# Turning B and C of the later pairs on TensorE instead of by DMA, in a fused state-space scan and bilinear feed-forward kernel

## The chip, the cores and the metric

One core of a Trainium2 chip. The metric is the device time of one execution in microseconds; the kernel before has a median of 124.77 us over three runs. An engine's work is named as the profile names it: PE is TensorE, DVE is VectorE, ACT is ScalarE, POOL is GpSimd, SP is SyncE.

## What is computed

Four batches of eight heads, 768 tokens each; x has 32 channels a head, B and C have 16 states. Blocked over tokens, the reference is

```python
cum = np.cumsum(log(a))                      # within a block of tokens
M   = (C_blk @ B_blk.T) * causal * exp(cum_i - cum_j)
y   = M @ x_blk + (C_blk @ state) * exp(cum_i)
state = exp(cum_last) * state + (B_blk * exp(cum_last - cum_j)).T @ x_blk
# heads side by side: 256 columns a token, 3072 tokens
out = ((y @ w_a) * (y @ w_b)) @ w_out        # 256 -> 1536 -> 256
```

## The kernel before

**Blocks and pairs.** A block is 128 tokens of all four batches; there are six (0 to 5). A pair is two of the four batches in one block, so pairs 0 to 11, two for each block; `P0 = 4` is the first pair of block 2 and `P2 = 8` the first of block 4. The decays are turned into factors for B and C (`fB`, `fC`, from TensorE's `factors_mm`, L254; for pairs from P2 on `fBl`, `fCl`, from VectorE's `late_factors`, L277), so that scores are plain products of scaled B (`bm`) and scaled C (`cm`). G, the decay over a block's border, comes from one matmul (L815).

**Rows.** Below P2 a partition holds two neighbouring tokens of one batch (`i r` in the code): B and C load in pieces of 128 bytes, x in 256. From P2 on a partition holds one token of both batches: pieces of 64 and 128 bytes, twice as many, loaded by one DMA for both batches (L163), not one for each (L154).

**A pair's way.** POOL scales B and C (`scale_bc`, L304 and L312). For the scores B and C must be turned, states to partitions, with odd and even heads of B in separate copies. Pairs 0 to 3 are turned by TensorE (`transposes`, four 128x128 transposes into PSUM, L334); ScalarE copies B twice, once for each head parity (`bt`, L345), VectorE copies C (`ct`, L346). Pairs 4 to 11 are turned by DMA (`turn`): POOL lays B's two parities and C out in a tile `planes` (L304, two copies at L322) and SP issues one transposing DMA from it (L356). Then come the scores (`scores`, L388, from P2 on L373), the causal mask (`mask`: three products on VectorE, one by ScalarE's copy `tmp` and POOL), the products with x and the part from the state, the sums for the next state (DS), and the copy to the feed-forward's input.

**Feed-forward.** Blocks 0 and 1 go pair by pair (`unit`: two k's of 128 hidden columns, four matmuls for `aps`, four for `bps`; ScalarE copies aps to `asb`, VectorE multiplies into `hk`; `out_half`: twelve matmuls and a copy `osb`). From block 2 on both pairs of a block go together: `group` does the state part (L523), products (L448 or L433) and DS (L475 or L462) of two pairs, ScalarE copies the result to `XB` (L553); `bunit` is one k with 512 columns (two matmuls each for aps and bps), `bout` one of four output halves (L709).

**What sets the order.** Everything is recorded in one hand-written order (`manual_schedule`); each engine takes its instructions in that order. PSUM has four banks for SC (scores, products, DS) and four that aps, bps, ops and the like share; a string `BANKS` gives, digit by digit, which of the four each new tile gets, so a tile waits until the copy of the tile before it in that bank is done. Input tiles have three buffers each (`inp`), output tiles ten. Loads stand on POOL's queue (weights with a cast, early pairs) and SP's (the rest); stores on SP. Stores of blocks 0 and 1 are collected in `stores` and issued at once in block 3. The order around the later blocks is

```python
masked(7, (0, 1, 2), *bu(2, 5, 6, 7, 8, 9, 10, 11))
group(3)
bout(2, 0)
bout(2, 1)
stage(8, True, (6, 7))        # scores(8), masks
...
masked(8, (2,), *bu(3, 0, 1, 2, 3, 4, 5))
for blk in range(4, NBLK):    # scores, bout(blk-2, 2), units 6 to 9, group(blk), bout(blk-2, 3), units 10, 11
```

Of the kernel before, what the change touches and what calls it, by code (L numbers as in the profile page):

```python
# [22 lines left out]
    "032130132013201320120310231023120132031203120132013201320310213021320310231023120130231023"  # L23
    "1021320312031203123021302130213021302130213021031203120312031203120312031203120312031"
# [4 lines left out]
def kernel(  # L29
# [28 lines left out]
    P2 = 8  # L58
# [4 lines left out]
    p32 = np.zeros((BH, 128 + nb * NG), np.float32)  # L63
    p32[:, 0:128] = (bh[:, None] % H) == (j[None, :] // N)
# [9 lines left out]
    c32 = const.tile([BH, p32.shape[1]], f32, name="c32")  # L74
# [5 lines left out]
    selb = c32[:, 128 : 128 + nb * NG]  # L80
# [8 lines left out]
    Wb = [big.tile([128, 2, KC], f16, name=f"Wb{t}") for t in range(2)]  # L89
# [7 lines left out]
    planes = [big.tile([128, 6, H * N], f16, name=f"planes{t}") for t in range(2)]  # L97
    causal_q = big.tile([128, Q], f16, name="causal_q")
    causal_r = big.tile([128, 2, Q], f16, name="causal_r")
# [5 lines left out]
    NL = NBLK - P2 // NBP  # L105
# [5 lines left out]
    hsx = big.tile([BH, nb, NG], f32, name="hsx")  # L111
    G = big.tile([128, nb, NG], f32, name="G")

    inp = ctx.enter_context(tc.tile_pool(name="inp", bufs=3))
# [31 lines left out]
    def load1(eng, p, which, bt, i0=0, n=64):  # L146
        blk, bp = divmod(p, NBP)
        if p >= P2:
            return eng.dma_start(
                by_token(pair_in[p][which])[:, bt],  # L150
                (B, C, x)[which][2 * bp + bt, :, blk * Q : (blk + 1) * Q, :].rearrange("h q n -> q h n"),
            )
        src = (B, C, x)[which][2 * bp + bt, :, blk * Q + 2 * i0 : blk * Q + 2 * i0 + 2 * n, :]
        return eng.dma_start(  # L154
            pair_in[p][which][64 * bt + i0 : 64 * bt + i0 + n].rearrange("i h r n -> i h (r n)"),
            src.rearrange("h (i r) n -> i h (r n)", r=2),
        )

    def load2(eng, p, which):
        if p < P2:  # L160
# [7 lines left out]
    def load_w(half):  # L168
        c = slice(half * KC, (half + 1) * KC)
        return [  # L170
            nc.gpsimd.dma_start(W[half], src.rearrange("(f p) e -> p f e", p=128)[:, :, c])
            for W, src in ((Wa, moe_w_a), (Wb, moe_w_b))
        ]
# [22 lines left out]
    nc.vector.memset(zero, 0.0)  # L196
    nc.gpsimd.memset(sel, 1.0)
# [22 lines left out]
    load_w(0)  # L220
# [48 lines left out]
    def late_rows(eng):  # L269
        k0 = P2 // NBP  # L270
# [14 lines left out]

    def scale_x(p, eng):
# [3 lines left out]
        if eng is nc.scalar:  # L290
# [4 lines left out]
    def scale_bc(p, which, eng, factor=None):  # L295
        blk, bp = divmod(p, NBP)
        name, f = (("bm", fB), ("cm", fC))[which]
        if p >= P2:
            f = (fBl, fCl)[which][:, blk - P2 // NBP].rearrange("p (b t h) -> p b t h", b=NBP, t=2)[:, bp]
        else:  # L300
            f = f[:, blk, :, bp]
        raw = by_token(pair_in[p][which]) if p >= P2 else pair_in[p][which].rearrange("p h r n -> p r h n")
        if p >= P0 and which:
            eng.tensor_tensor(  # L304
                out=planes[p % 2][:, 4:6].rearrange("p t (h n) -> p t h n", n=N),
                in0=raw,
                in1=f.unsqueeze(3).broadcast_to((128, 2, H, N)),
                op=ALU.mult,
            )
            return  # L310
# [8 lines left out]
        if p >= P0:  # L319
            dst = planes[p % 2][:, 0:4].rearrange("p (t e) (m f n) -> p t e m f n", e=2, f=2, n=N)  # L320
            for e in range(2):
                eng.tensor_copy(dst[:, :, e, :, e], m_.rearrange("p t (m f) n -> p t m f n", f=2)[:, :, :, e])  # L322

    def transposes(p, ps=None, between=None, apart=False):
        s = st[p]
        if ps is None:
            ps = [SC[0], SC[1]] if apart else None
            on_dve = apart
        else:
            on_dve = True  # L330
        TB, TC = (TT[:, 0:256], TT[:, 256:512]) if ps is None else [t_.bitcast(f16)[:, 0:256] for t_ in ps]
# [11 lines left out]
        for e in range(2):  # L343
            o_ = BT[:, e].rearrange("p r t i -> p (r t i)")
            b_.append(nc.scalar.activation(out=o_, in_=TB, func=AF.Copy, scale=par[:, e : e + 1]))  # L345
        c_ = (nc.vector.tensor_copy if on_dve else nc.scalar.copy)(  # L346
# [7 lines left out]
    def turn(p):  # L354
        T_ = mid.tile([128, 6, 128], f16, name="turned", tag="turned")
        nc.sync.dma_start(T_, planes[p % 2].rearrange("p a c -> p (a c)"), transpose=True)  # L356
        if p >= P2:
            st[p]["BT"] = T_[:, 0:4].rearrange("p (t e) k -> p e t k", e=2)
            st[p]["CT"] = T_[:, 4:6]
        else:  # L360
            st[p]["BT"] = T_[:, 0:4].rearrange("p (r e) (t i) -> p e r t i", e=2, t=2)
            st[p]["CT"] = T_[:, 4:6].rearrange("p r (t i) -> p t r i", t=2)

    def shaped(t_, p):
        return t_.rearrange("p (r i) -> p r i", r=2) if P0 <= p < P2 else t_

    def scores(p):
        BT, CT = st[p]["BT"], st[p]["CT"]
        st[p]["T1"] = mid.tile([128, H, 2, Q], f16, name="t1", tag="t1")
        for e, bt, m in itertools.product(range(2), range(2), range(4)) if p >= P2 else ():  # L370
# [11 lines left out]
        for e in range(2) if p < P2 else ():  # L382
            for r in range(2):
                for m in range(4):
                    for bt in range(2):
# [3 lines left out]
                            shaped(SC[m][64 * bt : 64 * bt + 64, c0 : c0 + Q], p),  # L389
# [8 lines left out]
    def product(p, m):  # L398

        if p >= P2:  # L400
# [8 lines left out]
            (causal_r if p >= P0 else causal).rearrange("p r q -> p (r q)").unsqueeze(1).broadcast_to((128, 2, 2 * Q)),  # L409
# [19 lines left out]
    def pv_u(p, u, py, first):  # L429
        s = st[p]  # L430
        for bt, g in itertools.product(range(2), range(4)) if p >= P2 else ():
# [10 lines left out]
        for r in range(2) if p < P2 else ():  # L442
            for g in range(4):
                for bt in range(2):
                    h = u * 4 + g
                    k = slice(64 * bt, 64 * bt + 64)
                    c0 = 32 * (g ^ 2 * bt) if p >= P0 else 32 * g
                    nc.tensor.matmul(  # L448
                        py[bt, u][c0 : c0 + 32] if p >= P0 else py[bt][c0 : c0 + 32, u * Q : (u + 1) * Q],
# [8 lines left out]
    def ds_mm(p, c0, banks):  # L458
        s = st[p]
        s["DS"] = [b_[:, c0 : c0 + 2 * D] for b_ in banks]  # L460
        for bt, m in itertools.product(range(2), range(4)) if p >= P2 else ():
# [9 lines left out]
        for r in range(2) if p < P2 else ():  # L471
# [41 lines left out]
    def outputs(blk):  # L513
# [3 lines left out]
        for j, p in enumerate(pairs):  # L517
            s = st[p]
            for m in range(4):
                for bt in range(2):  # L520
# [3 lines left out]
                        shaped(SCt[bt][half : half + 64, m // 2, cols[j]], p),  # L524
# [86 lines left out]
    def unit_mm(p, k2, W):  # L611
        ps = bank("aps" if W is Wa else "bps")
        for kk in range(2):
            k = 2 * k2 + kk
            for f in range(2):
                nc.tensor.matmul(  # L616
                    ps[:, kk * 2 * Q : (kk + 1) * 2 * Q],
                    W[k // 6][:, f, k % 6 // 3 * 384 : (k % 6 // 3 + 1) * 384].rearrange("p (c kk) -> p kk c", kk=3)[
                        :, k % 3
                    ],  # L620
# [20 lines left out]
    def unit(p, k2, between=None):  # L641
        a_ps = unit_mm(p, k2, Wa)
        if between:
            between()
        b_ps = unit_mm(p, k2, Wb)
        asb = evac_a(a_ps)
# [14 lines left out]
    def out_store(p, bt, o_ps):  # L661
# [4 lines left out]
        stores.append(lambda: nc.sync.dma_start(out[r0 : r0 + Q, :], o_sb))  # L666

# [6 lines left out]
    def bunit(blk, k):  # L674
# [4 lines left out]
        for W in (Wa, Wb):  # L679
            t_ = bank("aps" if W is Wa else "bps")  # L680
            for f in range(2):
                nc.tensor.matmul(  # L682
                    t_,
                    W[k // 6][:, f, k % 6 // 3 * 384 : (k % 6 // 3 + 1) * 384].rearrange("p (c kk) -> p kk c", kk=3)[
                        :, k % 3
                    ],
# [13 lines left out]
    def bout(blk, c, parts=1):  # L700
# [4 lines left out]
        for part in range(parts):  # L705
# [16 lines left out]
            if blk * NBP < P2:  # L722
                for r, half in enumerate(rows.rearrange("(i r) d -> r i d", r=2)):
                    nc.sync.dma_start(half, o_sb[64 * r : 64 * r + 64])
            else:
                (nc.sync, nc.scalar)[part].dma_start(rows[:, cs], o_sb[:, 0:w])

    def loads_bc(p):
        if p < NP:
            tiles(p)  # L730
            for w in (1, 0):
                load2(nc.sync, p, w)
# [5 lines left out]
    def fb(k):  # L738
        if k * NBP >= P2:
            nc.vector.reciprocal(fBl[:, k - P2 // NBP], fCl[:, k - P2 // NBP])  # L740
# [45 lines left out]
    for bt in range(2):  # L786
        evac0(1, bt, (nc.scalar, nc.vector)[bt], py)
    scan(4, 5)
    w1 = load_w(1)
# [4 lines left out]
    sel_over_mid(1, P2 // NBP, nc.vector)  # L794
# [3 lines left out]
        out=hsx,  # L798
# [4 lines left out]
    for bt in range(2):  # L803
        load1(nc.gpsimd, 2, 0, bt)
# [3 lines left out]
    scores(1)  # L808
    mask(product(1, 3), by_pool=True)
# [264 lines left out]
```

## Time and profile before

| | |
|---|---|
| median of three runs | 124.77 us (124.35 to 125.11) |
| the profiled execution's own time | 125.18 us |
| its span, first to last instruction | 123.4 us |
| granted TensorE clock | 0.998 |
| asb<-aps, ACT, 128x512 | 587 ns each, 72 times |
| hkb<-bps,asb, DVE, 128x512 | 688 ns each, 48 times |
| turned<-planes, DMA transposition | 8, 3.5 us from issue to landing |
| out_dram<-osb | 33 DMAs |

The 1.8 us between the span and the time lie outside the program's instructions. In a row of the page or of a group, the numbers after the bar are busy time and the mean of one in ns, then the engine's idle time before them and what ended it. A timeline row has start, length, engine, line, operation, tiles and count; what stands in square brackets is the idle time of the engine before it. The starts tell the pace: instructions of one engine overlap somewhat, matmuls by far.

### The profile page before, as it was taken

The numbers are of one execution on the slowest core, as the hardware profiler recorded it, in microseconds if no ns is written. First come the engines' busy times: TensorE is split into PE (matmuls) and PEld (weight loads), VectorE is DVE, ScalarE is ACT, GpSimd is POOL, SyncE is SP. The second block draws the span as 40 slices with busy tenths as digits, with TensorE's granted clock in tenths as the row PEclk, the third lists the DMA queues.
The fourth block names the chain that finished last, engine by engine and source line by source line (L and its number), as shares of the span: only waits on it lengthen the run. The fifth ranks groups of instructions, "written<-read, shape, count | busy, mean of one in ns | idle before, by whom it ended". The sixth has DMA issues, their size and how long they took to land.

```text
span 123.4 us, 4060 instructions
## 1 busy us (share of the span) xinstructions
PE 118.6 (96%) x1615; PEld 80.6 (65%) x1615; DVE 86.8 (70%) x167; ACT 71.4 (58%) x141; POOL 61.6 (50%) x108
## 2 busy tenths in 40 slices
PE   5999999999999999999999999999999999999990
PEld 2446798878898888744467455757464785555890
DVE  1787889794968898498973989847889444847100
ACT  0466756856364784887657756664637736556220
POOL 7999997955776339297590895025900000000000
PEclk9999999999999999999999999999999999999999
DMA  2999999975657858979999685689643012010122
GB/s 62 160 159 235 156 194 169 206 103 112 100 91 171 99 94 94 152 107 125 92 147 125 57 232 172 119 82 159 114 112 66 0 43 90 0 42 0 42 86 84
DMA packets 54770, 13.75 MB, mean 111 GB/s; under 512 B 49648, under 2 KB 54416, under 8 KB 54752
## 3 DMA queue, kind: packets, MB, share of 16 engines
q1 hardware_dynamic: 50624, 9.53, 48.5%
q0 software_dynamic: 2128, 3.61, 16.5%
q10 hardware_dynamic: 2000, 0.36, 1.6%
q8 instruction: 12, 0.20, 0.7%
q14 instruction: 6, 0.05, 0.2%
HBM read 11.13 MB, written 3.15 MB: 116 GB/s over the span
## 4 chain that ended last, share of the span: by engine, by line
PE 72%; DMA 16%; POOL 3%; DVE 3%; issue 2%; ACT 2%; POOLq 0%; ACTq 0%
PE ops L709 15%; PE aps L682 15%; PE bps L682 14%; PE ops L652 7%; DMA Wb<-in_moe_w_b_dram 7%; DMA xn<-in_x_dram 6%; PE aps L616 4%; PE bps L616 4%; PE SC L226 4%; DMA turned<-planes 3%; PE SC L388 2%; DVE hkb L694 2%; PE SC L448 1%; POOL bm L312 1%; PE SC L373 1%
## 5 line engine op out<-in xcount | busy, mean ns | idle before, releaser
L630 ACT COPY asb<-aps 128x512 f32<-128x512 f32 x72 | 42.0, 587 | 14.5 <-PE aps L682 9.6
L694 DVE TENSOR_TENSOR hkb<-bps,asb 128x512 f16<-128x512 f32 x48 | 32.3, 688 | 12.9 <-ACT asb L630 11.8
L682 PE MATMUL aps<-XB,Wa 128*128 128x512 f16 x96 | 28.6, 379 | 0.0
L682 PE MATMUL bps<-XB,Wb 128*128 128x512 f16 x96 | 28.5, 379 | 0.0
L709 PE MATMUL ops<-Wo,hkb 128*128 128x256 f16 (+1 forms) x204 | 22.5, 267 | 0.0
L709 PEld LDWEIGHTS <-hkb 128*128 128x128 f16 x204 | 18.5, 98 | 3.1
L637 DVE TENSOR_TENSOR hk<-bps,asb 128x512 f16<-128x512 f32 x24 | 16.2, 687 | 2.4 <-ACT asb L630 1.7
L682 PEld LDWEIGHTS <-Wb 128*128 128x128 f16 x96 | 9.9, 103 | 11.0 <-issue 0.2
L682 PEld LDWEIGHTS <-Wa 128*128 128x128 f16 x96 | 9.7, 103 | 9.1 <-issue 0.2
L721 ACT ACTIVATE osb<-ops 128x256 f32<-128x256 f32 (+1 forms) x16 | 6.0, 377 | 14.3 <-PE ops L709 14.2
L616 PE MATMUL aps<-X2T,Wa 128*128 128x256 f16 x96 | 14.3, 273 | 0.0
L616 PE MATMUL bps<-X2T,Wb 128*128 128x256 f16 x96 | 14.3, 273 | 0.0
L652 PE MATMUL ops<-Wo,hk 128*128 128x256 f16 x96 | 11.6, 273 | 0.0
L427 DVE TENSOR_TENSOR t<-SC,causal_q 128x512 f16<-128x512 f32 x15 | 9.5, 681 | 1.8 <-PE SC L373 1.8
L616 PEld LDWEIGHTS <-Wa 128*128 128x128 f16 x96 | 9.5, 103 | 1.2 <-DMA Wa<-in_moe_w_a_dram 0.3
L616 PEld LDWEIGHTS <-Wb 128*128 128x128 f16 x96 | 9.6, 103 | 0.9 <-DMA Wb<-in_moe_w_b_dram 0.3
L293 POOL TENSOR_SCALAR x<-xn 128x512 f16<-128x512 f32 x6 | 9.0, 1493 | 2.3 <-DMA xn<-in_x_dram 2.0
L652 PEld LDWEIGHTS <-hk 128*128 128x128 f16 x96 | 8.9, 98 | 1.5 <-DVE hk L637 0.2
L427 DVE TENSOR_TENSOR t<-SC,causal_r 128x512 f16<-128x512 f32 x12 | 7.8, 682 | 2.0 <-PE SC L388 2.0
L427 DVE TENSOR_TENSOR t<-SC,causal 128x512 f16<-128x512 f32 x13 | 8.2, 683 | 1.0 <-PE SC L388 0.9
L553 ACT ACTIVATE XB<-SC 64x512 f16<-64x512 f32 (+1 forms) x9 | 5.3, 594 | 3.5 <-PE SC L475 2.5
L425 POOL TENSOR_TENSOR t<-tmp,causal_r 128x512 f16<-128x512 f32 x4 | 4.6, 1162 | 5.0 <-ACT tmp L424 4.9
(102 smaller groups left out, 128.9 us busy)
## 6 DMA issues: line engine op xcount, KB each, us to landing
out_dram<-osb SPq DMA_DIRECT2D x15, 128.0 KB, 1.8
xn<-in_x_dram SPq DMA_DIRECT2D x11, 128.0 KB, 4.0
out_dram<-osb SPq DMA_DIRECT2D x17, 64.0 KB, 2.0
bn<-in_B_dram SPq DMA_DIRECT2D x12, 64.0 KB, 2.9
Wa<-in_moe_w_a_dram POOLq DMA_DIRECT2D x2, 384.0 KB, 6.5
Wb<-in_moe_w_b_dram POOLq DMA_DIRECT2D x2, 384.0 KB, 7.7
Wo<-in_moe_w_out_dram POOLq DMA_DIRECT2D x2, 384.0 KB, 7.8
xn<-in_x_dram SPq DMA_DIRECT2D x3, 256.0 KB, 5.1
```

The costliest lines, as they stand in the source:

```text
L226: nc.tensor.matmul(bank[:, 0:cols], warm[:, 0:128], warm[:, 0:cols], start=True, stop=True, skip_group_check=True)
L293: eng.tensor_scalar(xo, xi, XS, None, ALU.mult)
L427: nc.vector.tensor_tensor(out=o_, in0=i_, in1=c_, op=ALU.mult)
L553: nc.scalar.activation(out=XB[to, blk - P0 // NBP, :, bt].rearrange("p u j q -> p u (j q)"), in_=SCt[bt][fr, :, 0 : NBP * Q], func=AF.Copy ...
L616: nc.tensor.matmul(ps[:, kk * 2 * Q : (kk + 1) * 2 * Q], W[k // 6][:, f, k % 6 // 3 * 384 : (k % 6 // 3 + 1) * 384].rearrange("p (c kk) -> ...
L630: (nc.vector.tensor_copy if on_dve else nc.scalar.copy)(asb, a_ps)
L637: nc.vector.tensor_tensor(out=s["hk"][:, 2 * k2 : 2 * k2 + 2, :].rearrange("p k q -> p (k q)"), in0=b_ps, in1=asb, op=ALU.mult)
L652: nc.tensor.matmul(o_ps[:, 0:d_model], hk[:, k, bt * Q : (bt + 1) * Q], Wo[:, k, :], start=(k == 0), stop=(k == NK - 1), skip_group_check= ...
L682: nc.tensor.matmul(t_, W[k // 6][:, f, k % 6 // 3 * 384 : (k % 6 // 3 + 1) * 384].rearrange("p (c kk) -> p kk c", kk=3)[:, k % 3], XB[:, b ...
L694: return lambda: nc.vector.tensor_tensor(out=s["hk"][:, k], in0=ps[1], in1=asb, op=ALU.mult)
L709: nc.tensor.matmul(o_ps[:, 0:w], hk[:, k, c * Q : (c + 1) * Q], Wo[:, k, cs], start=(k == 0), stop=(k == NK - 1), skip_group_check=True,)
L721: nc.scalar.activation(out=o_sb[:, 0:w], in_=o_ps[:, 0:w], func=AF.Copy, scale=1.0 / (YS * YS))
```

## The change

`P2` goes: from pair 4 on every pair has one-token rows and factors from `late_factors` (VectorE's transposes of a tile twice as wide), so `factors_mm` makes block 1's factors alone, and outputs of blocks 2 and 3 are stored by one DMA, not two. `turn` and `planes` go: from pair 4 on `transposes` turns B and C on TensorE into a bank of the shared four (named `tr`), and ScalarE copies all three parts out. `transposes(4)` stands behind pair 3's products, `transposes(5)` behind pair 4's scores, 6 and 7 behind `group(2)` (7 after an `out_half`), 8 and 9 behind `group(3)` (9 after a `bout`), 10 behind `group(4)`, 11 after `bout(3, 0)`. Input tiles get nine buffers, and SP issues the loads of x for pairs 4 and 5 and all loads of pairs 6 to 11 in one run behind pair 3's scores; pair 4's B and C are issued by POOL behind pair 2's scaling. Stores of pairs 0 and 1 wait for pair 2's, then each is issued as it comes, behind that run on SP. Wb is loaded in three parts, G's matmul is split in four behind pair 1's DS, x of pair 2 is scaled half by ScalarE and half by VectorE, x of pairs 4 and 5 by POOL, and `BANKS` is another string.

```diff
-    planes = [big.tile([128, 6, H * N], f16, name=f"planes{t}") for t in range(2)]
-    NL = NBLK - P2 // NBP
+    NL = NBLK - P0 // NBP
+    WC = (KC // 2, KC // 2, KC)
+    Wb = [big.tile([128, 2, w], f16, name=f"Wb{t}") for t, w in enumerate(WC)]
-    inp = ctx.enter_context(tc.tile_pool(name="inp", bufs=3))
+    inp = ctx.enter_context(tc.tile_pool(name="inp", bufs=9))
...
     def transposes(p, ps=None, between=None, apart=False):
         s = st[p]
-        if ps is None:
+        if p >= P0:
+            ps = [bank("tr").bitcast(f16)] * 2
+            TB, TC = ps[0][:, 0:256], ps[0][:, 256:512]
+            on_dve = False
+        elif ps is None:
...
             b_.append(nc.scalar.activation(out=o_, in_=TB, func=AF.Copy, scale=par[:, e : e + 1]))
+        if p >= P0:
+            nc.scalar.copy(CT.rearrange("p t q -> p (t q)"), TC)
+            s["BT"], s["CT"] = BT.rearrange("p e r t i -> p e r (t i)"), CT
+            return
...
-    def turn(p):
-        T_ = mid.tile([128, 6, 128], f16, name="turned", tag="turned")
-        nc.sync.dma_start(T_, planes[p % 2].rearrange("p a c -> p (a c)"), transpose=True)
...
     def unit(p, k2, between=None):
         a_ps = unit_mm(p, k2, Wa)
+        asb = evac_a(a_ps)
         if between:
             between()
         b_ps = unit_mm(p, k2, Wb)
-        asb = evac_a(a_ps)
...
+        if p > 1:
+            store_all()
...
-    w1 = load_w(1)
+    w1 = [load_w(Wb, 1), load_w(Wa, 1), load_w(Wb, 2)][1:]
...
-    for bt in range(2):
-        load1(nc.gpsimd, 2, 0, bt)
...
     scores(1)
+    fps = bank("fps")
+    factors_mm(1, P0 // NBP, fps)
     mask(product(1, 3), by_pool=True)
+    for bt in range(2):
+        load1(nc.gpsimd, 2, 0, bt)
...
-    bps = [unit_mm(0, k2, Wb) for k2 in range(2)]
+    bps = [unit_mm(0, 0, Wb)]
...
     ds_mm(0, 64, SC[:2])
-    bps.append(unit_mm(0, 2, Wb))
+    gps = SC[0][:, 256 : 256 + nb * NG]
+    for c in range(4):
+        nc.tensor.matmul(
...
+    bps += [unit_mm(0, k2, Wb) for k2 in range(1, 3)]
...
     scale_bc(2, 0, nc.gpsimd)
-    for t_ in planes:
-        nc.gpsimd.memset(t_[:, 0:4].bitcast(u32), 0)
     scale_bc(2, 1, nc.gpsimd)
+    loads_bc(4, nc.gpsimd)
+    nc.gpsimd.memset(causal_q, 1.0)
...
     mask(product(2, 3), by_pool=True)
+    late_rows(nc.gpsimd)
...
     out_store(0, 0, o[0])
+    out_mm(0, 1, o[1], range(6, NK))
+    out_store(0, 1, o[1])
     pull(2)
     pv(2, split=True)
-    out_mm(0, 1, o[1], range(6, NK))
-    out_store(0, 1, o[1])
+    out_half(1, 0)
+    state_sums(2)
     h = unit(2, 0, lambda: transposes(3, apart=True))
-    state_sums(2)
+    h()
+    late_factors()
     fb(2)
...
     prep(4, (2,))
-    loads_x(4, nc.sync)
-    loads_x(5, nc.sync)
-    prep(5)
-    loads_bc(6)
-    loads_bc(7)
+    for p in range(4, NP, 2):
+        if p > 5:
+            loads_bc(p)
+            loads_bc(p + 1)
+        loads_x(p, nc.sync)
+        loads_x(p + 1, nc.sync)
...
     group(2)
+    transposes(6)
     out_half(3, 0)
+    transposes(7)
     out_half(3, 1)
...
     group(3)
+    transposes(8)
     bout(2, 0)
+    transposes(9)
     bout(2, 1)
...
         group(blk)
+        if blk + 1 < NBLK:
+            transposes(pB + 1)
         bout(blk - 2, 3)
...
             masked(pB + 1, (2,))
+            transposes(pB + 2)
             bout(blk - 1, 1)
```

## The prediction

> **What bounds the kernel now.** I read the page's first two parts, then the chain of waits, then the timelines of single engines around the places that the change touches.
>
> The page's busy shares and slices:
>
> ```profile
> PE 118.6 (96%) x1615; PEld 80.6 (65%) x1615; DVE 86.8 (70%) x167; ACT 71.4 (58%) x141; POOL 61.6 (50%) x108
> ...
> PE   5999999999999999999999999999999999999990
> ...
> PEclk9999999999999999999999999999999999999999
> ```
>
> TensorE is the bound from the second slice to the last, at its full granted clock. The ends of matmuls are modelled, so I take its cost from the distance between starts: in the timeline a matmul of 512 columns starts 0.216 us after the one before, one of 256 columns 0.109 us, one of 128 columns 0.055 us. Added TensorE work therefore costs its full length, and a gain elsewhere counts only where TensorE waits today. The chain shows the largest such wait of the middle stages, pair 8's, among its rows of groups 2 to 4 (start, length, what):
>
> ```profile
> 47.34 0.25 PE SC L523 x16
> 47.59 0.82 PE SC L448 x62
> 48.41 0.27 PE SC L475 x29
> ...
> 67.07 0.05 issue
> 67.12 0.40 PE SC L373 x16
> ...
> 72.87 0.33 PE SC L373 x16
> ...
> 78.32 0.56 PE SC L433 x32
> 78.88 0.12 PE SC L462 x16
> ```
>
> A DMA transposition ends at 67.07 and only then the scores of pair 8 start; in the timeline the output matmuls before them ended their issue some 0.2 us earlier. So the DMA transpositions, 3.5 us each in the list of DMA issues, are nearly all hidden today.
>
> **TensorE's own work.** A pair's four transposes, and what one of ScalarE's copies behind them takes:
>
> ```profile
> 22.61 0.28 PE L334 MATMUL SC<-ident,bm 128*128 128x128 f16 x2
> 22.72 0.28 PE L334 MATMUL SC<-ident,cm 128*128 128x128 f16 x2
> 22.83 0.60 PE L616 MATMUL aps<-X2T,Wa 128*128 128x256 f16 x4
> ...
> L345 ACT ACTIVATE bt<-SC,ch 128x256 f16<-128x256 f16 x6 | 2.5, 471 | 0.7 <-PE SC L334 0.6
> ```
>
> From 22.61 to 22.83 is 0.22 us for four. Eight pairs get them: +1.76. The Trainium skill (VectorE: DVE Perf Modes, The three transpose paths) gives 390 ns for a 128x128 transpose by TensorE and 1309 ns by DMA; taken as occupancy its 390 ns would make the 32 cost 12.5 us, but the rows start 55 ns apart, so it is at most a latency, and the sum goes by the row.
>
> One-token rows make the scores of pairs 4 to 7 16 matmuls (0.33) in place of 32 (0.36): -0.12. The products and state sums of a block shrink from 0.82 + 0.27 (group 2) to 0.56 + 0.12 (group 4), -0.41, in two blocks: -0.82. Factors of blocks 2 and 3 leave TensorE: L254 takes 24 passes in 0.82 us (13.15 to 13.97), 8 remain: -0.55. The matmul for G becomes four, moved behind pair 1's state sums in their tile shape; eight passes of 0.034 against 0.33 now: -0.05. Sum: +0.2. TensorE's own work is as good as unchanged.
>
> **Waits that go.** Pair 8's wait, -0.2. The upper half of Wb is now wanted later: bps starts at 19.44 after an aps at 18.86 (0.58 for a usual 0.44), the next after 0.55: -0.25. Pair 2's x, scaled in two halves (the timeline has 0.19 before L448 at 27.68): -0.2. Sum -0.65.
>
> **Waits that come, early.** POOL sets both. Its timeline now:
>
> ```profile
> 14.05 1.20 POOL L425 TENSOR_TENSOR t<-tmp,causal 128x512 f16<-128x512 f32 x1
> ...
> 20.39 0.64 POOL L312 TENSOR_TENSOR bm<-bn,fB 128x256 f16<-128x256 f32 x1
> 20.96 0.57 POOL L839 MEMSET planes<- 128x256 uint32 x2
> 21.48 0.63 POOL L312 TENSOR_TENSOR cm<-cn,fC 128x256 f16<-128x256 f32 x1
> 22.06 1.16 POOL L588 TENSOR_TENSOR sbd<-U,maskbd 128x512 f16<-128x512 f32 x1
> ...
> 25.89 1.16 POOL L425 TENSOR_TENSOR t<-tmp,causal 128x512 f16<-128x512 f32 x1 [0.84 <-ACT tmp L424]
> ```
>
> Pair 1: three weight DMAs in place of two before hr (0.74 more), but the two loads of B (1.44) move behind the mask, so the mask runs 13.3 to 14.5. TensorE reaches the second half of pair 1's products, which needs it, earlier: 14.99 less 0.55 (factors), 0.33 (G) and 0.44 (a unit moved behind), plus 0.18 for the first half, is 13.85. It waits to 14.55: +0.7, and the factors' gain is given back.
>
> Pair 2: from 20.39 POOL does bm and cm to 21.6, then issues pair 4's two loads with 2048 descriptors each (the one such issue on POOL, L163, takes 1.23), to 24.1, makes causal_q (0.5), spreads two states (3.0, from 22.06 to 25.05 now), to 27.6, and masks to 28.7; now it ends at 27.05. TensorE comes to the second half of pair 2's products at 27.86 + 0.65 (six output matmuls moved ahead) - 0.45 (the two waits above) + 0.1, 28.15: +0.6. Bounds for the two together: 0.3 to 1.8.
>
> Behind that mask POOL has Ps, twice as wide (1.2 for 0.6), pair 3's bm and cm (1.25), its x (1.5) and pair 4's cm and bm (1.25): ready at 31.1, 32.6 and 33.9. All of TensorE stands behind a transpose that waits: pair 3's comes at about 31 (0.1 at most), pair 4's at 36.6. VectorE's part of pair 4, four fCl transposes now twice as wide (0.97 for four today) and a reciprocal (0.35), follows its product near 32 and also ends in time.
>
> **Waits that come, at ScalarE.** Each turned pair asks ScalarE for three copies: two bt of 471 ns (0.84 for both in the timeline) and ct, between an osb copy of the same size (381) and a bt. Back to back a copy costs about 0.1 less than its length: 1.1 us a pair. Pairs 4 and 5 stand between units; their copies hold back asb, so a bank or the output matmuls wait some tenths: +0.3 (0 to 0.6). Pairs 6 to 10 stand right behind a group, where ScalarE is latest. Group 4's end now:
>
> ```profile
> 79.04 1.90 ACT L553 ACTIVATE XB<-SC 128x512 f16<-128x512 f32 x3 [0.78 <-PE SC L462]
> 80.96 0.38 ACT L721 ACTIVATE osb<-ops 128x256 f32<-128x256 f32 x1
> 81.24 1.15 ACT L630 COPY asb<-aps 128x512 f32<-128x512 f32 x2
> ```
>
> XB first, to 80.94, then the three copies, to 82.0. TensorE: transposes from 79.0, output half 1.42, unit 10, and at 81.5 it wants a bank for unit 11. BANKS gives it the bank of tr, free at 82.05: 0.6. The same count for group 3 (XB to 66.23 in the timeline, then tr, osb, tr, osb, tmp, asb): the first asb ends at 69.85, and unit 2 wants its bank at 69.5; with 0.1 at the scores, 0.45. For group 2: XB ends at 50.64, the first asb at 54.3 for a want at 54.05, and some 0.15 at the banks before: 0.4. Sum +1.45; bounds 0 (the units behind have slack of their own) and 2.4 (ct as long as bt, 0.1 more at each copy and place). VectorE, 70% busy, has no more to do there but follows asb. POOL loses L322's 16 copies (4.7 us) and takes x of pairs 4 and 5; nobody waits for it in that stage.
>
> **Loads.** SP's stores now stand behind all loads. Pairs 4 to 7 move 64-byte pieces. Rows of SP's timeline:
>
> ```profile
> 78.53 0.57 SPq L163 DMA_DIRECT2D cn<-in_C_dram x1
> 79.15 2.05 SPq L163 DMA_DIRECT2D bn<-in_B_dram x1
> 81.25 3.03 SPq L163 DMA_DIRECT2D xn<-in_x_dram x2
> ```
>
> From about 27.6 SP has 14 loads of B or C and 8 of x: at 2.05 and 1.6 us, 41.5, done near 69. The eleventh output copy, near 76, needs the first store landed, 3 us after SP gets there. So about 4 us of cover; I cost the loads at nothing.
>
> **Sum.** 0.2 - 0.65 + 1.3 + 0.3 + 1.45 = +2.6; 0.1 less for short waits of TensorE on VectorE now near 55 and 61: +2.5. The profiled execution took 125.18 with a span of 123.4 (1.8 outside), 0.4 above the median 124.77. So a profiled execution of 127.7, and a median of 127.3.
>
> **Rivals.** *The copies fit.* If ScalarE ends its copies half a microsecond earlier at each group, and POOL's mask of pair 2 by 28.15, only 0.2 - 0.65 + 0.7 + 0 is left, 125.0; without pair 1's wait too, 124.2. It decides at 81.5 in group 4: bank free or not. For it: ScalarE is 58% busy. Against: just there it works without a gap from 79.04 on. The Trainium skill (VectorE: DVE Perf Modes, Rules for kernel authors) prefers TensorE for a 128x128 transpose where PSUM may take the result; this rival is the time by that rule, and the trace bears it out only for TensorE's own 0.22 us. To be measurably faster it also needs VectorE's waits to go, below 124.15.
>
> *Stores too late.* At 2.5 us a load of B or C, as the worst rows before 61 us suggest (2.19, 2.25, 2.53), SP is 6.3 us later, 2 past the cover; output copies hold ScalarE and TensorE: about 129. It decides at 2.3 us a load. The Trainium skill (DMA: Bandwidth & Descriptors, Specifications) wants 512 bytes and more for line rate; the trace agrees that smaller pieces cost more, 2.05 for 128 KB in 64-byte pieces against 0.68 for 64 KB in 128-byte ones (issues from 42.2 to 45.6).
>
> *Only half of ScalarE's waits*, 126.4: inside my range. That the change does not do what it says is no rival: in the order of instructions the eight DMA transpositions are gone and 32 transposes stand on TensorE.
>
> **Numbers.** Forecast 127.3, chance 0.6; half the waits 0.14; stores late 0.1; copies fit 0.16, half of it measurably faster; the rest of "same" is the low end of the half waits. About 0.5%, 0.6 us, is what can be told from no change. Faster 0.08, same 0.12, slower 0.8. The range, 124.6 to 129.3, takes in the copies that fit and most of the late stores.
>
> **What would show it.** TensorE's transposes at 0.22 a pair; pair 1's and 2's second halves waiting on POOL; aps waiting on ct or asb after groups 2, 3 and 4, some 0.4 to 0.6 each; no wait at 67. I am wrong if these waits are missing, or if another one, on loads or osb, is larger.

## The result and the profile after

The changed kernel takes 129.16 us (four executions: 128.62, 128.63, 129.69, 130.0) against 124.88 us for the kernel before: ratio 1.0355, 95% interval 1.0277 to 1.0433. Run again it took 130.37 us (129.51 to 130.65): ratio 1.0434 (1.0387 to 1.0481). So it is slower, by 4.3 to 5.6 us; the forecast was +2.5. Its executions do not agree among themselves: two at 128.6, the other six between 129.5 and 130.7. The execution profiled first is a short one (128.62, span 126.9), the one profiled in the second run a long one (130.45, span 128.7). All ratios leave out executions that lie more than 1.5% above the fastest of their kernel; below, that concerns two of turn_out's nine (128.17 us at full clock, 129.43 us at a clock of 0.987) and single ones of the kernel before.

The changed kernel's page, first two parts:

```profile
PE 119.0 (94%) x1477; PEld 81.2 (64%) x1477; DVE 87.1 (69%) x169; ACT 77.7 (61%) x164; POOL 62.6 (49%) x94
...
PE   6999799979989999999999999979999999999991
```

TensorE is busy as long as before (119.0 for 118.6 us) in fewer instructions, though it now makes 32 transposes more: its work is unchanged, as the sum had it. What is new are the slices of 7 and 8 in the PE row. ScalarE has 6.3 us more work (77.7 for 71.4). What TensorE waits for in the short execution (engine, tile and line, what ended the wait; us in total, times, longest), besides 1.2 us at the very start that the kernel before has too:

```profile
PE SC L444 <- POOL t L421: 0.9, 1, 0.9
PE SC L444 <- DVE t L423: 0.8, 1, 0.8
PE aps L678 <- ACT ct L352: 0.8, 1, 0.8
PE aps L678 <- ACT asb L624: 0.5, 2, 0.2
PE SC L488 <- DVE t L423: 0.3, 1, 0.3
```

The first two are pair 2's and pair 1's products, the next two the first units behind the groups, the last pair 3's products. Pair 8's scores no longer wait at 67, and neither a store nor a load of pairs 4 to 11 appears. By distances between starts, less the usual distance, the places cost more than the list shows: 1.0 us before pair 1's products (13.3), 1.1 in the middle of pair 2's (27.7), 0.5 at pair 3's (35.9), 0.24 at an output half (40.4), 0.39, 0.39 and 0.98 at aps (54.8, 70.8, 83.4). Starts of the same stage, after less before, show where it adds up: -0.41 at scores of pair 2, +1.26 at those of pair 4, +1.49 at `group(2)`, +1.86 at `group(3)`, +2.24 at `group(4)`, +3.66 at `group(5)`.

Group 4's end on ScalarE (the row that the forecast's 0.6 was counted from):

```profile
81.28 0.60 ACT L549 ACTIVATE XB<-SC 128x512 f16<-128x512 f32 x1 [0.78 <-PE SC L458]
82.19 1.20 ACT L549 ACTIVATE XB<-SC 64x512 f16<-64x512 f32 x2 [0.32 <-DVE U L576]
83.39 0.84 ACT L350 ACTIVATE bt<-tr,ch 128x256 f16<-128x256 f16 x2
84.12 0.37 ACT L352 COPY ct<-tr 128x256 f16<-128x256 f16 x1
84.38 0.41 ACT L715 ACTIVATE osb<-ops 128x256 f32<-128x256 f32 x1
```

ScalarE first idles 0.78 us, until the group's products are done, then does XB, the three copies and osb in one row, and TensorE's second aps behind the group waits for the ct in it, to 84.55.

What the long execution has more stands in the second run's profile. TensorE and POOL of the changed kernel, run again:

```profile
30.68 0.28 PE L339 MATMUL SC<-ident,bm 128*128 128x128 f16 x2
32.85 0.29 PE L339 MATMUL SC<-ident,cm 128*128 128x128 f16 x2 [1.89 <-POOL cm L317]
```

```profile
21.38 1.23 POOL L162 DMA_DIRECT2D cn<-in_C_dram  x1
22.56 1.21 POOL L162 DMA_DIRECT2D bn<-in_B_dram  x1
...
27.27 1.15 POOL L421 TENSOR_TENSOR t<-tmp,causal 128x512 f16<-128x512 f32 x1
28.39 1.09 POOL L275 TENSOR_TENSOR Ps<-Pr,rmid 32x512 f32<-32x512 f32 x1
29.44 0.61 POOL L317 TENSOR_TENSOR bm<-bn,fB 128x256 f16<-128x256 f32 x1
32.17 0.62 POOL L317 TENSOR_TENSOR cm<-cn,fC 128x256 f16<-128x256 f32 x1 [2.12 <-DMA cn<-in_C_dram]
```

In the middle of pair 3's transposes TensorE stands for 2.05 us (distance between starts), because POOL can scale pair 3's C only when its second half has landed, at 32.04. In the short execution that half landed at 30.18, just in time for a scaling at 30.36; in the kernel before at 27.85. The two L162 rows are pair 4's loads of C and B. The change moved them from SP to POOL, ahead of the mask, and they are in flight beside pair 3's. What the DMA queues moved between 25 and 28 us (packets, MB, share of the 16 engines' time; q0 carries POOL's loads, q1 SP's, as the difference between the two executions shows), first in this execution, then in bc4_on_sp below, which issues both loads on SP:

```profile
q1 hardware_dynamic: 1563, 0.20, 70.2%
q0 software_dynamic: 84, 0.25, 60.0%
...
q1 hardware_dynamic: 2159, 0.37, 86.1%
q0 software_dynamic: 11, 0.02, 2.7%
```

### The profile page after: what moved, and what is told of

Its sections match the earlier page's. It is cut to its first block, busy times and chain, and to the rows that moved or that the text cites. A ratio compares the mean times of both kernels' runs of the same rounds, so it can differ in the third digit from the quotient of the medians.

```text
span 126.9 us, 3758 instructions
## 1 busy us (share of the span) xinstructions
PE 119.0 (94%) x1477; PEld 81.2 (64%) x1477; DVE 87.1 (69%) x169; ACT 77.7 (61%) x164; POOL 62.6 (49%) x94
## 4 chain that ended last, share of the span: by engine, by line
PE 63%; ACT 12%; POOL 9%; DMA 6%; issue 4%; DVE 4%; ACTq 0%; POOLq 0%; DVEq 0%
PE aps L678 15%; PE bps L678 15%; PE ops L703 14%; DMA Wb<-in_moe_w_b_dram 6%; PE ops L646 4%; ACT bt L350 3%; PE aps L612 3%; PE SC L230 3%; ACT XB L549 2%; PE bps L612 2%; POOL sbd L584 2%; DVE hk L631 2%; ACT asb L624 2%; PE SC L369 2%; PE SC L429 1%
## 5 line engine op out<-in xcount | busy, mean ns | idle before, releaser
L678 PE MATMUL aps<-XB,Wa 128*128 128x512 f16 x96 | 28.6, 379 | 1.3 <-ACT ct L352 0.8
L423 DVE TENSOR_TENSOR t<-SC,causal_q 128x512 f16<-128x512 f32 x27 | 17.4, 682 | 6.1 <-PE SC L369 5.5
L421 POOL TENSOR_TENSOR t<-tmp,causal_q 128x512 f16<-128x512 f32 x5 | 5.8, 1161 | 16.3 <-ACT tmp L420 16.3
L306 POOL TENSOR_SCALAR x<-xn 128x512 f16<-128x512 f32 x8 | 11.9, 1491 | 1.8 <-DMA xn<-in_x_dram 1.2
L423 DVE TENSOR_TENSOR t<-SC,causal 128x512 f16<-128x512 f32 x12 | 7.6, 678 | 1.0 <-PE SC L384 0.9
L420 ACT COPY tmp<-SC 128x512 f32<-128x512 f32 x9 | 5.4, 599 | 2.4 <-PE SC L384 1.1
```

The costliest lines, as they stand in the source:

```text
L306: eng.tensor_scalar(xo, xi, XS, None, ALU.mult)
L421: nc.gpsimd.tensor_tensor(out=o_, in0=tmp, in1=c_, op=ALU.mult)
L423: nc.vector.tensor_tensor(out=o_, in0=i_, in1=c_, op=ALU.mult)
L678: nc.tensor.matmul(t_, w_up(W, k, f), XB[:, blk - P0 // NBP, f].rearrange("p t j q -> p (t j q)"), start=(f == 0), stop=(f == 1), skip_gro ...
```

## The experiments

Each ratio is to the kernel before on the same chip, with its 95% interval. Runs under one heading share a chip. Where a kernel leaves out part of the computation, its time serves for the comparison alone.

### First set: the change again, ScalarE's copies out, the transposes out, the rows alone

**again**: the changed kernel, unaltered.

> The changed kernel once more, unaltered: its four times lay at 128.6 (twice), 129.7 and 130.0. If the 1.2 us between them come from the order in which loads land, the traces of a short and a long execution should differ at one early wait (pair 3's inputs, pair 4's), and be parallel after it; if they come from TensorE's pace, all stages should be longer by one factor (0.9%).

130.37 us, ratio 1.0434 (1.0387 to 1.0481). The waits of the first profile are there, all but one in nearly the same size, and the 2.05 us of pair 3's C besides, shown above. The exception is pair 2's: 0.8 in place of 1.1 us, and what ends it is VectorE's half of x (28.6), POOL's mask having ended at 28.4. From pair 3's scores on the two executions are parallel: 1.8 us apart there, at pair 4's scores and at every group.

**copies_out**: in `transposes`, before the copies:

```diff
+        if p >= 6:
+            s["BT"], s["CT"] = st[5]["BT"], st[5]["CT"]
+            return
```

> The changed kernel; for pairs 6 to 11 the transposes are issued, but ScalarE's three copies are left out, and the scores take pair 5's turned B and C. Theory (ScalarE's copies behind a group keep the shared banks): the waits of aps at 55.4, 71.4 and 84.5 go, 0.39 + 0.39 + 0.97, 1.75 us shorter than the changed kernel. Rival (the transposes' own time on TensorE is the cost): less than 0.3 us shorter.

127.73 us, ratio 1.0218 (1.0176 to 1.026): 2.6 us less than the kernel again. The three waits at aps are gone and none replaces them: from the start of pair 5's scores to that of `group(5)` TensorE takes 52.36 us, where the changed kernel takes 54.36 in both its profiles, 2.0 less. The two profiled executions are 1.9 apart; here pair 3's transposes waited 1.7 us, not 2.05. The rest of the 2.6 is in no trace.

**turn_out**: those lines stand ahead of the transposes (with the bank's digit still taken), so that the 24 transposes of pairs 6 to 11 go too.

> As copies_out, and the 24 transposes of pairs 6 to 11 are left out too. Both theories: 6 x 0.22 = 1.3 us shorter than copies_out, if TensorE is the bound in these stages. If it is less than 0.6 shorter, something else sets their pace.

126.21 us, ratio 1.011 (1.0067 to 1.0153). That is 1.5 us less by medians, 1.35 by ratios, but with these intervals anything from 0.6 to 2.1, and the early part differs too: in this profile pair 3's transposes do not wait. The starts settle it: from pair 5's scores to `group(5)` it is 51.07 us, 1.29 less than in copies_out, against 1.3 from 0.22 a pair. So a transpose costs TensorE 54 ns, the distance between starts, and not a latency. The Trainium skill (VectorE: DVE Perf Modes, The three transpose paths) has 390 ns; by that figure, as an estimate, 24 of them would have been 9.4 us.

**rows_alone**: the kernel before with `P2 = 4` (one-token rows and VectorE's factors from pair 4 on; the DMA goes on turning).

> The kernel before with one part of the change alone: one-token rows from pair 4 on (P2 = 4), factors of blocks 2 and 3 by VectorE, their rows made by POOL ahead of pair 2's mask and turned by VectorE behind pair 2's products; turning stays with the DMA, three input buffers, loads and banks as before. Theory: TensorE loses 0.82 (products, state sums), 0.12 (scores) and 0.55 (factors); with the last given back to pair 1's mask 0.9 shorter than before, up to 1.5. Rival (the slower loads in 64-byte pieces, or VectorE's longer factor work ahead of pair 3, are the cost of the change): as long as before or longer by up to 2 us.

124.45 us, ratio 0.9983 (0.9952 to 1.0013): the expected 0.9 to 1.5 did not come. TensorE has less to do, but comes to pair 2's products earlier than their inputs: it waits 0.85 us at 27.0, where the kernel before waits 0.36, for x of pair 2, which lands at 27.24 behind Wo in the same queue. Later the saving does come: from pair 5's scores to `group(5)` it is 51.15 us for 52.22 before, 1.07 less. Of that the early part takes 0.2 and the time behind the last matmul another 0.2 (the profiled spans are 122.8 and 123.4).

### Second set: pair 4's loads, VectorE's factors, the rows once more

**bc4_on_sp**:

```diff
-    loads_bc(4, nc.gpsimd)
...
     loads_x(3, nc.sync)
+    loads_bc(4)
     loads_bc(5)
```

> After, with pair 4's loads of B and C issued by SP, between pair 3's x and pair 5's B and C, and not by POOL behind pair 2's scaling. Theory: these two loads cost twice: POOL spends 2.35 us on issuing them ahead of the mask of pair 2, and what they move lands beside pair 3's inputs, so that pair 3's C comes late in most executions. Then TensorE's wait in the second half of pair 2's products falls from 1.1 us to under 0.2, and pair 3's transposes no longer wait 2.05 us for C: against a time of after around 129.5 (128.6 to 130.7), -1.0 for the first and -1.0 to -2.0 for the second, so 126.8 to 127.5. Rival, the early part is bound by the bytes that have to land, whoever issues them: the loads of pairs 4 and 5 on SP come later and the wait moves to pair 3's or pair 4's inputs, and the time falls by POOL's 1.0 at most, to 128.5.

128.31 us, ratio 1.0278 (1.0248 to 1.0308): 1.0 to 2.0 us less than the change in its two runs, and six executions within 1.1 us. POOL in this kernel:

```profile
20.96 0.61 POOL L317 TENSOR_TENSOR cm<-cn,fC 128x256 f16<-128x256 f32 x1
...
25.23 1.16 POOL L421 TENSOR_TENSOR t<-tmp,causal 128x512 f16<-128x512 f32 x1 [0.17 <-ACT tmp L420]
26.34 1.03 POOL L275 TENSOR_TENSOR Ps<-Pr,rmid 32x512 f32<-32x512 f32 x1
27.55 0.62 POOL L317 TENSOR_TENSOR bm<-bn,fB 128x256 f16<-128x256 f32 x1 [0.17 <-DMA bn<-in_B_dram]
28.12 0.62 POOL L317 TENSOR_TENSOR cm<-cn,fC 128x256 f16<-128x256 f32 x1
```

The mask of pair 2 ends at 26.4, not 28.4 to 28.8, and pair 3's C has landed by 27.96. Neither pair 2's wait nor the one for pair 3's C is in the list any more, and pair 4's own inputs (30.55 and 31.78) still come before POOL wants them. Pair 5's scores start at 43.55, 1.26 us earlier than in the short execution and 3.08 earlier than in the long one, and behind them nothing changes (54.34 us to `group(5)`). So the theory held in its mechanism, and the rival's (the wait goes to the inputs of pairs 3 or 4) fell. The time did not follow: it is not the expected 126.8 to 127.5 but near the rival's 128.5. The profiled execution (127.72) is the shortest of the six, part of the changed kernel's executions had no 2.05 to lose, and what the other five (128.2 to 128.8) wait for is in no trace.

**bc4_and_factors**: besides, `late_factors()` stands ahead of the unit that holds pair 3's transposes.

```diff
+    late_factors()
     h()
-    late_factors()
```

> As the kernel with pair 4's loads on SP, and VectorE's late factors moved ahead of the unit that holds pair 3's transposes, from behind it. Theory: in after the three masks that VectorE makes for pair 3 stand behind four transposes of 1.24 us and a reciprocal of 0.35, and TensorE waits 0.5 in pair 3's products; ahead of the unit VectorE has the time, and that wait goes: -0.4 against the kernel with the loads alone, 126.4 to 127.0. Rival: the loads and the masks of pair 3 are one chain, and with pair 3's B and C in time the wait for the masks is gone already: no difference, within 0.15.

127.56 us, ratio 1.0238 (1.0204 to 1.0272): half a microsecond less by ratios, whose intervals overlap. By the starts the 0.5 is there: from pair 3's scores to pair 4's it is 8.63 us, not 9.12, and the wait of 0.5 at pair 3's products is gone. The time missed the expected 126.4 to 127.0, since the kernel with the loads alone was slower than assumed. VectorE in the changed kernel (first profile), where it was:

```profile
32.47 1.24 DVE L281 STREAM_TRANSPOSE fCl<-Ps 32x128 f32<-32x128 f32 x4
33.74 0.35 DVE L730 RECIPROCAL fBl<-fCl 128x32 f32<-128x32 f32 x1
34.01 0.63 DVE L423 TENSOR_TENSOR t<-SC,causal 128x512 f16<-128x512 f32 x1
...
35.15 1.28 DVE L423 TENSOR_TENSOR t<-SC,causal 128x512 f16<-128x512 f32 x2
```

**rows_alone_out_first**: the rows alone, with the last six output matmuls of pair 0's second half ahead of pair 2's products.

```diff
+    out_mm(0, 1, o[1], range(6, NK))
+    out_store(0, 1, o[1])
     pull(2)
     pv(2, split=True)
     late_factors()
-    out_mm(0, 1, o[1], range(6, NK))
-    out_store(0, 1, o[1])
```

> The kernel before with one-token rows from pair 4 on (late factors on VectorE, DMA still turning B and C), as run already, and besides the last six output matmuls of pair 0's second half and their copy moved ahead of pair 2's products, as the change has them. In the run of the rows alone TensorE waits 0.85 us there for pair 2's x, which lands at 27.2 behind the weights (0.36 in the kernel before). Theory: 0.65 us of matmuls that are ready fill that wait, and the rows' gain comes out: 0.6 to 0.7 faster than the rows alone, 123.7 to 123.9. Rival: ScalarE's copy of those outputs now stands ahead of its part of pair 2's x or of pair 2's result, and the wait stays: 124.4.

124.48 us, ratio 0.9974 (0.9957 to 0.9991). The wait for x is filled, but those matmuls had covered what stands behind the products: the next aps now waits 0.75 us at 28.3, for VectorE's copy of pair 2's result. The gain of the theory did not come, and the rival's time is right for another reason than it gave. From pair 5's scores to `group(5)` it is 51.14 us, as in rows_alone.

### Third set: where the copies stand, the rows again, pair 1's mask

**turned_ahead**: the kernel of bc4_and_factors, with the transposes of pairs 6, 8 and 10 ahead of the groups. The banks stay as they are.

```diff
+    transposes(6)
     group(2)
-    transposes(6)
...
+    transposes(8)
     group(3)
-    transposes(8)
...
+        if blk + 1 < NBLK:
+            transposes(pB + 1)
         group(blk)
-        if blk + 1 < NBLK:
-            transposes(pB + 1)
```

> The kernel with pair 4's loads on SP and the late factors early, and the transposes of pairs 6, 8 and 10 (with ScalarE's copies) moved from behind the groups to right ahead of them. Theory: behind a group ScalarE is latest because the XB copies, the turned pair's three and osb stand in one row; in the group itself it waits some 0.8 us for TensorE. Ahead of the group 0.8 of the 1.1 us of copies falls into that time: the waits of aps at about 53.3, 69.3 and 81.8 (0.39, 0.39, 0.98) go to under 0.1 each, and TensorE waits at most 0.3 for the scaled B of pair 6. -0.9 to -1.6: 126.0 to 126.7 against 127.56. Rival: the copies hold back the last asb of the block, or VectorE's products behind it, so that the next output half waits as long: 127.3 to 127.8.

126.23 us, ratio 1.0101 (1.0066 to 1.0136): 1.7 us less than 1.0238, none of the three waits is left. The starts say the same: from pair 5's scores to `group(5)` 52.66 us for 54.37, 1.71 less. ScalarE at group 4:

```profile
78.15 0.84 ACT L350 ACTIVATE bt<-tr,ch 128x256 f16<-128x256 f16 x2
78.88 0.37 ACT L352 COPY ct<-tr 128x256 f16<-128x256 f16 x1
79.13 0.62 ACT L549 ACTIVATE XB<-SC 128x512 f16<-128x512 f32 x1
79.99 1.19 ACT L549 ACTIVATE XB<-SC 64x512 f16<-64x512 f32 x2 [0.24 <-DVE U L576]
81.21 0.38 ACT L715 ACTIVATE osb<-ops 128x256 f32<-128x256 f32 x1
```

The idle 0.78 is filled with copies, and the row from XB to osb is 1.0 us shorter. TensorE waits 0.24 us ahead of pair 6's transposes at 46.9 instead. The size is what the expectation allowed, the cause is not: pair 6's scaled B is done at 45.3, and by the chain of waits it ends with VectorE's `hk` product, at 47.25, which presumably frees the bank. What the same copies still cost, one step earlier in the order, copies_out_2 shows.

**rows_both_outs**: rows_alone_out_first, with pair 1's first output half moved too, right behind pair 2's products (and the banks of six tiles changed to suit).

> The kernel before with one-token rows from pair 4 and pair 0's outputs ahead of pair 2's products (run already), and besides pair 1's first output half moved from block 2's first units to right behind pair 2's products, as the change has it. In the run before it TensorE waited 0.75 there, at 28.3, for VectorE's copy of pair 2's result. Theory: twelve ready output matmuls (1.3 us) cover that wait, and what the one-token rows save reaches the end: -0.6 to -0.8, 123.7 to 123.9, measurably faster than the kernel before. Rival: the wait comes back where the output half is taken from, at pair 3's products or the units around them, which wait for VectorE's masks: 124.3 to 124.6.

125.23 us, ratio 1.0021 (0.9996 to 1.0045): the rival, and worse than it said. The wait comes back where the output half was taken from: pair 3's products wait 1.3 us at 34.6 for VectorE's masks. But its profile also has 0.6 us of waiting for Wa near 11 us, ahead of everything that the edit touches, and that is part of "worse". Three kernels with the rows alone, and three waits of 0.75 to 1.3 us at three different places of the early part, which loses 0.2 to 1.2 us up to pair 5's scores; behind that all three gain the same 1.07 to 1.08.

**wb_behind_mask**: the kernel of bc4_and_factors, with Wb's third part issued by POOL behind pair 1's mask.

> The kernel with pair 4's loads on SP and the late factors early, and the third part of Wb issued by POOL behind its mask of pair 1, not ahead of it. The forecast put pair 1's wait (1.0 us before its products, at 13.3) on this mask, behind three weight loads. Theory: VectorE's three masks end at the same time (14.3, POOL's at 14.25), because scores(1) comes before; the wait stays 0.9 to 1.0, and the time 127.4 to 127.7. Rival, POOL alone sets it: the mask ends 0.7 earlier, TensorE's wait falls to 0.3, and the time to 126.9.

128.22 us, ratio 1.0258 (1.0211 to 1.0304). Pair 1's wait stays, at 1.0 us. POOL's mask cannot come forward, for it begins at 13.04 anyway, when ScalarE's `tmp` is there, and VectorE's three masks end no sooner:

```profile
12.39 1.89 DVE L423 TENSOR_TENSOR t<-SC,causal 128x512 f16<-128x512 f32 x3 [0.65 <-PE SC L384]
```

So this wait comes from scores(1), as the theory said, and not from the weight loads. The time is not lower but 0.2 (by ratios, whose intervals overlap) to 0.7 us (by medians) higher, outside what was expected: Wb now lands late, and bps waits 0.6 us for it at 19.4.

### Fourth set: what the copies still cost, and pair 1's scores

**copies_out_2**: the lines of copies_out in the kernel of bc4_and_factors.

> The kernel with pair 4's loads on SP and the late factors early, with ScalarE's three copies of pairs 6 to 11 left out (their transposes stay, their scores take pair 5's turned B and C): part of the computation is missing. Its 0.39, 0.39 and 0.98 us of waits on ScalarE should go, and nothing comes in their place: -1.75, ratio 1.010 to the kernel before where the one with the copies had 1.0238. Theory: with the transposes right ahead of the groups ScalarE's copies cost nothing any more, so this kernel is no faster than that one (1.0101), within 0.4 us. Rival: the copies still cost something ahead of the groups that the list of waits does not name, 0.5 us or more: then it comes to 1.006 or less.

125.74 us, ratio 1.0065 (1.0031 to 1.0098), against 1.0238 with the copies behind the groups and 1.0101 with the transposes ahead. So behind the groups the copies cost 2.2 us, with three of the six pairs ahead of them some 0.4, just between what theory and rival said; by ratios, whose intervals overlap, whether anything is left cannot be told. The starts tell it: from pair 5's scores to `group(5)` 54.37 us with the copies behind the groups, 52.66 with the transposes ahead and 52.36 without copies. The copies cost 2.0 us behind the groups and 0.3 ahead of them.

**scores_earlier**: turned_ahead, with pair 1's scores between the two aps units.

```diff
-    aps = [unit_mm(0, 0, Wa), unit_mm(0, 1, Wa)]
+    aps = [unit_mm(0, 0, Wa)]
     asb = [evac_a(aps[0])]
     scores(1)
+    aps.append(unit_mm(0, 1, Wa))
```

> The kernel with the transposes of pairs 6, 8 and 10 ahead of the groups, and besides pair 1's scores ahead of the second of the two units' matmuls, not behind both. If VectorE's three masks of pair 1 set the wait before its products (1.0 us at 13.1), they start some 0.4 earlier and TensorE waits 0.4 less net of the copies that scores(1) needs. Theory: the end gains less than that, 0 to 0.3, since TensorE then comes that much earlier to the weights and inputs which land at 19 to 27 us: the early part is bound by what has landed, and the wait shows again at the unit at 19.5 or at pair 2's products. Rival, VectorE's masks are the bound of that part: -0.4, ratio 1.007.

125.85 us, ratio 1.0076 (1.0041 to 1.0111). Pair 1's wait falls from 1.0 to 0.36 us, and the one for pair 2's x grows from 0.28 to 0.44; the profiled executions have the same span, 123.9. The gain of 0.3 by ratios is what the theory allowed and the ratio 1.0076 is also near the rival's 1.007; each of the two kernels' ratios lies in the other's interval. By the starts pair 5's scores come 0.08 us earlier, which speaks for the theory, from one execution each.

## Why the prediction was half right

**Right: slower, and why TensorE does not gain.** Transposes of 0.22 us a pair (1.29 for six pairs by the starts), no wait left at 67, TensorE's busy time as before. In the changed kernel SP ends its loads at 63.5, earlier than the 69 counted, and no output copy waits for a store: the rival of the late stores is refuted. That its 129 is near the measured time is chance.

**Right: ScalarE behind the groups, 1.45, with one size off.** Groups 2 and 3 cost 0.39 each (0.4 and 0.45 forecast), pairs 4 and 5 0.24 (0.3); by the starts of the stages, the copies of pairs 6 to 11 cost 2.0 in all. Group 4 cost 0.98 where 0.6 was counted. The step took XB's three copies as one block of 1.9 us; in the run the second waits 0.32 for VectorE's U (L576), so all behind it is later. The Trainium skill (TensorEngine Tiling (Array Packing), PSUM Bottleneck) says that, where tiling makes TensorE four times faster, copies out of PSUM may become the bottleneck, and that both ScalarE and VectorE should be used for them. Here TensorE is no faster, but the trace agrees that the copies were dearer than the transposes, 2.0 against 1.29 us for six pairs. No run tried the sharing; the runs show another answer, the same engine before the group.

**Wrong in one cause, its size right by luck: the early waits, 1.3.** Pair 1 lost 1.0 us against 0.3 before, the forecast's +0.7. It named POOL's mask, behind three weight loads; wb_behind_mask shows that without the third load the wait stays. Four things end there within 0.3 us (ScalarE's x at 14.02 and fC at 14.10, POOL's mask at 14.25, VectorE's masks at 14.31), and all stand behind scores(1); with scores(1) earlier the wait fell to 0.36. The size fits because two errors offset each other: TensorE came at 13.4, not 13.85, and the inputs were there at 14.3, not 14.55. Pair 2's wait is POOL's in the short execution, as forecast: POOL's mask ended at 28.8 (28.7 forecast), but TensorE was there at 27.7, not 28.15, so 1.1 and not 0.6.

**Wrong: "I cost the loads at nothing".** This is the step that failed. It counted when SP would come through its run, and looked there for harm to stores. Of pair 4's two loads it counted only POOL's issue time, 2.5 us (2.35 measured), and not what they move: 256 KB that land beside pair 3's 512 KB. For pair 3's transposes, "pair 3's comes at about 31 (0.1 at most)" took POOL's queue alone; pair 3's C, landed at 27.85 before, lands at 30.18 in the short execution and at 32.04 in the long one, which costs nothing in the one and 2.05 us in the other. In the long execution that is most of what it has above the forecast, and the 1.8 us between the two profiles come from it. The forecast's own sign of being wrong, a wait on loads that is larger than the others, is there. Of the four profiles of kernels with pair 4's loads on POOL (changed kernel twice, copies_out, turn_out) two have this wait, 2.05 and 1.7 us; of the six with these loads on SP none has it, and C has landed by 27.96 to 29.15. That the executions without a profile differ by the same wait is presumed, not shown.

The Trainium skill (DMA: Bandwidth & Descriptors, Queues, rings and completion order) says that each DMA engine takes turns between its queues, packet by packet. By that rule a transfer issued later on POOL's queue takes its share from an earlier one on SP's; the trace agrees in the landings (POOL's C, issued at 21.38, landed at 30.43; SP's second C of pair 3, issued at 21.60, at 32.04; with both on SP, pair 3's B and C landed by 27.96 and pair 4's at 30.55 and 31.78). The bytes by queue, shown above, agree too: 0.25 MB on POOL's queue in the 3 us in which SP's moved 0.20, for 0.02 and 0.37 with both loads on SP. The order of the turns is not in them, nor why the short execution, with nearly the same bytes (0.24 and 0.19), had its C 1.9 us sooner.

**Missing: pair 3's masks, 0.5.** The step on VectorE's late factors said that it "also ends in time", and looked at pair 4, which wants them. It did not look at what is queued behind them: 1.6 us of transposes and reciprocal ahead of pair 3's masks, for which TensorE waits. bc4_and_factors gave it back. In the short execution, where the loads cost nothing, this 0.5 and the 0.4 of group 4 are about what the profile has above the forecast (+3.4 for +2.5).

**The sum.** In ratios: 1.0355 to 1.0434 as it was; pair 4's loads on SP, 1.0278; the factors early, 1.0238; the copies ahead of the groups, 1.0101. TensorE's starts in the profiles split it in two (us):

| kernel | pair 5's scores start | `group(5)` starts | between |
|---|---|---|---|
| before | 43.29 | 95.51 | 52.22 |
| changed, short execution | 44.81 | 99.17 | 54.36 |
| changed, long execution | 46.63 | 100.99 | 54.36 |
| bc4_on_sp | 43.55 | 97.89 | 54.34 |
| bc4_and_factors | 43.26 | 97.63 | 54.37 |
| turned_ahead | 43.18 | 95.84 | 52.66 |
| copies_out_2 | 44.13 | 96.49 | 52.36 |
| turn_out | 44.89 | 95.96 | 51.07 |
| rows_alone | 43.52 | 94.67 | 51.15 |

From the start of `group(5)` to that of the last matmul all take 24.67 us. The part between repeats to 0.03 us wherever the kernels agree there: 1.15 us saved (rows, pair 8's wait), 1.29 spent on transposes, 2.0 on copies. The part up to pair 5's scores is where the loads act, and it varies from execution to execution. By these starts turned_ahead's last matmul is 0.3 us later than that of the kernel before, by medians the kernel is 1.26 slower; the profiled execution is its shortest, and what the others wait for is not known. None of the versions that turn on TensorE reaches the kernel before: its DMA transpositions cost TensorE 0.2 us in all. The best of all, the rows alone with pair 0's outputs first, is 0.3 us faster (0.9974), below what the forecast called measurable.

## What to carry to other kernels

When a load is moved to another queue, count it three times: the issue time on the engine that now issues it, who is queued behind it there, and which transfers of other queues it will be in flight with; the last can cost most, and here it showed as a spread between executions. Before new work is put on an engine that is 60% busy, find where that engine idles in the stage itself: 1.1 us of copies cost 0.4 to 1.0 each time behind a group; with the transposes of three pairs moved ahead of the groups all six pairs' copies cost 0.3. A gain in a stage that is bound by landing data can come out as a wait a few microseconds later, as it did in three kernels here, so look for the last arrival first.

## What the runs showed of the hardware

With loads of two queues in flight, the time of issue did not tell the landing: the same program, with loads issued within 0.7 us of the same times, had pair 3's C landed at 30.18 in one execution and 32.04 in another. And the loads of one-token rows were somewhat faster than the kernel before suggested: SP's run of 14 loads of B or C (64-byte pieces) and 8 of x took 36.6 us to issue (26.87 to 63.47 in the first profile), 1.66 us a load, where the durations picked from rows of before make 1.89. The forecast had picked 2.05 for B and C; the row beside it, a load of the same size, has 0.57.
